# Two expert ranks fixed after two of four batches, their weights prepared beside the third mixing, units handed out three times, and their rows loaded by plain transfers

## The chip, the cores and the metric

The kernel runs on one core of a Trainium2 chip. The metric is the device time of one execution in microseconds (us); the median of three runs is shown below. An engine is a part of the core with an instruction queue of its own, worked off strictly in order: PE multiplies matrices, DVE and ACT do elementwise work, POOL issues transfers with lists of row numbers (indirect transfers), SP issues plain transfers and transposing transfers. An engine whose next instruction waits holds everything queued behind it.

## The reference

Two stages. The first is an attention over channels, for 4 batches of 5056 tokens and 256 channels; the second is a mixture of 8 experts in which each token goes to the one expert with the largest gate.

```python
qn = q / (norm(q, axis=1) + 1e-6);  kn = k / (norm(k, axis=1) + 1e-6)   # B=4, N=5056, C=256
s = kn.transpose(0, 2, 1) @ qn / tau          # 256 x 256 for each batch
a = softmax(s, -1);  x = v @ a                # rows of x are the 20224 tokens
e_idx = argmax(x @ w_gate, 1)                 # one of 8 experts for each token
out[mask] = gate_w * sigmoid(x @ w_output_gate)[e] * (relu(x[mask] @ w1[e]) @ w2[e])   # mask: e_idx == e
```

w1 is 8 x 256 x 1024 and w2 is 8 x 1024 x 256. The experts' load is known only once the gates are computed.

## The kernel before

**Gram and mixing.** For each batch, `gram` loads q and k in tiles of 128 x 512 (tile `qk`, six buffers), multiplies them into `s_ps` (L341), adds up squares (ACT L328, DVE L329), and ends in a short softmax. `mix` then goes through the batch in 5 groups of 4 steps: each step turns a tile of v on PE (`vt_ps`, L456), copies it out (`vh` on ACT L460, `vl` on DVE L462) and multiplies (`x_ps`, L479 to L481; copied to `st` by ACT L482). A group has 16 turned blocks (of 128 x 128) and 48 products of `x_ps`. After a group, `route` picks the expert of each token with some 18 small DVE instructions, counts places with nine small PE products (`r_ps`, L540 and L543), and scatters the 1024 rows by eight indirect transfers (POOL L559) into `xs_d`, a list in DRAM with a region for each expert. `rc` holds the number of tokens that each expert has so far.

**Weights.** `prep` fetches an expert's weights by indirect transfer (`raw`, POOL L245, 1 MB for w1 and 1 MB for w2, called halves here), in the order of rank: rank 0 is the expert with the most tokens when the ranks are fixed. `split` takes the square (ACT L268, two pieces into the buffer of `whi`), sums it on PE (`w_ps`, L273), makes a scale from it (DVE), and writes a high part `whi` (ACT L290, four pieces for w1 and two for w2) and a low part `wlo` (DVE L291), which SP stores to `wsc` in DRAM (L297).

**Units.** A unit is 256 tokens (or 128) of one expert. `table` lays down for each unit where its rows lie (`gi`) and which weight rows it needs (`wi`). `open_marks` reads a mark behind the scatters, so that `gi` is known only when they have landed. `fetch_x` loads a unit's rows (`xg`, L781), `fetch_w` its weights (`wbuf`, L768, 1 MB for each half, two buffers), `prepare` scales the rows (ACT L826, DVE L827) and has SP transpose them (`xt`, L831). PE multiplies 48 times for the first layer (`h_ps`, L850 to L852; out by ACT L854 and DVE L855 to `hb`) and 48 times for the second (`y_ps`, L873 to L875); ACT writes `yo`, POOL scatters it to the output (L885). There are 72 whole units and 21 halves.

**Order.** The main part interleaves generators: `_beside(main, (gen, rate))` makes `rate` steps of `gen` for each of `main`. The order of each engine's queue then comes from a scheduler that weighs the instructions of these steps. Before the change: the grams run beside the mixings of batches 0 to 2; after the third mixing the ranks are fixed and 10 units handed out, and ranks 0 and 1 are prepared beside the first 14 steps of the last mixing; the units start beside its end; after it the other 83 units are handed out and ranks 2 to 7 prepared beside the units.

```python
for b in range(B - 1):
    _beside(mix(b), (ahead, GRATE))
early = checkpoint(False)
next(early)
preps = prep(0, 2, "raw")
tail = mix(B - 1)
```

Of the kernel before, what the change touches and what calls it, by code (L numbers as in the profile page):

```python
# [20 lines left out]
P = 128  # L21
# [5 lines left out]
def _beside(main, *others):  # L27

    due = [0.0 for _ in others]
    for _ in main:  # L30
        for i, (gen, rate) in enumerate(others):
            due[i] += rate
            while due[i] >= 1.0:
                due[i] -= 1.0
                next(gen, None)


@with_exitstack
def tile_colnorm_attention_then_top1_moe(
# [37 lines left out]
    EARLY = 10  # L77
# [5 lines left out]
    SURE = -(-((B - 1) * N - E * (BLK - 1)) // BLK)  # L83
    FIRST = [-(-r * SURE // E) for r in range(E)]
    assert EARLY <= FIRST[2] and EARLY + LATER - NHALF >= FIRST[E - 1]
# [32 lines left out]
    PRATE = 1  # L118
    ALONE = 14
    LATE = 7  # L120
    BRATE = 1.0
    WRATE = 0.45
# [70 lines left out]
    mark = cst.tile([P, 2], I32, name="mark")  # L193
# [42 lines left out]
    def prep(first, end, tag):  # L236
        todo = []
        for r in range(first, end):
            for half in range(2):
                if tag == "st":  # L240
                    raw = wk.tile([P, R, CW], F32, tag="st", name=f"raw{r}_{half}", bufs=STB)
                    raw = raw.rearrange("p r w -> p (r w)")[:, :HW1]
                else:
                    raw = big.tile([P, HW1], F32, tag="raw", name=f"raw{r}_{half}", bufs=3)
                nc.gpsimd.indirect_dma_start(  # L245
                    out=raw,
                    out_offset=None,
                    in_=wraw[half],
                    in_offset=bass.IndirectOffsetOnAxis(ap=ri[:, r : r + 1], axis=0),
                    bounds_check=E * P - 1,  # L250
                    oob_is_err=False,
                )
                todo.append(lambda raw=raw, half=half, r=r: split(raw, half, r))
                yield
                if len(todo) > 1:
                    yield from todo.pop(0)()
        for f in todo:
            yield from f()
# [175 lines left out]
    def mix(b):  # L434
# [5 lines left out]
        def turn(j):  # L440
# [20 lines left out]
            vl = wk.tile([P, CC, 2 * P], F32, tag="vl", name="vl", bufs=XTB).bitcast(F32R)  # L461
# [236 lines left out]
    def rank_experts():  # L698
# [288 lines left out]
```

## Time and profile before

| what | value |
|---|---|
| median of three runs (lowest, highest) | 1265.51 us (1261.57, 1273.47) |
| the profiled execution | 1272.18 us, of which the profile's span is 1270.5 us |
| granted PE clock over the span | 0.98 |
| PE busy | 1204.7 us (95%), 10708 matmul records |
| DVE, ACT, POOL busy | 735.6, 629.5, 655.8 us |
| bytes moved | 211.46 MB, mean 166 GB/s |

The span begins with the first instruction. The grams and the first three mixings run to about 286 us, the last mixing and the first units to about 400 us, and units fill the rest. A record is one pass through PE: a product of `s_ps` has two, the other large ones one.

### The profile page before, as it was taken

How to read it: one execution, taken by the hardware profiler on the slowest of the kernel's cores; microseconds unless marked ns; L12 is line 12 of the kernel's file. 1: busy time of each engine (PE TensorE's matmuls, PEld its weight loads, DVE VectorE, ACT ScalarE, POOL GpSimd, SP SyncE). 2: the span in 40 equal slices, each digit the busy share in tenths (PEclk: the TensorE clock that was granted, in tenths of full speed). 3: DMA queues.
4: the chain of work that ended last, by engine and by line, in shares of the span. 5: the costliest groups of instructions: out<-in, count | busy, mean ns of one | idle time of the engine just before them, and what ended most of it. 6: DMA issues, size and time to landing. Idle time of an engine off the chain costs nothing.

```text
span 1270.5 us, 28599 instructions
## 1 busy us (share of the span) xinstructions
PE 1204.7 (95%) x10708; PEld 1092.5 (86%) x10708; DVE 735.6 (58%) x2235; ACT 629.5 (50%) x1231; POOL 655.8 (52%) x643
## 2 busy tenths in 40 slices
PE   7999999996669999999999999899999999999996
PEld 6899898995668788888888888788899999999996
DVE  5767767766678466565656666444445555555431
ACT  4676666664755456455554645333333444334332
POOL 0005665667577754555555544344455555555442
PEclk9999999998879999999999999999999999999999
DMA  9877787857697765565565546933263333465520
GB/s 333 277 251 243 244 276 230 270 179 228 218 329 181 190 159 167 120 143 144 144 143 144 143 111 159 180 70 73 64 176 107 78 78 79 114 212 165 161 59 17
DMA packets 176418, 211.46 MB, mean 166 GB/s; under 512 B 125352, under 2 KB 127022, under 8 KB 171032
## 3 DMA queue, kind: packets, MB, share of 16 engines
q1 hardware_dynamic: 124568, 100.73, 29.4%
q0 software_dynamic: 51712, 108.92, 29.3%
q8 instruction: 84, 1.38, 0.5%
q14 instruction: 54, 0.44, 0.1%
HBM read 296.94 MB, written 61.80 MB: 282 GB/s over the span
## 4 chain that ended last, share of the span: by engine, by line
PE 81%; DMA 9%; DVE 3%; ACT 2%; issue 2%; POOL 1%; SPq 0%; POOLq 0%; ACTq 0%; DVEq 0%
PE h_ps L850 10%; PE h_ps L852 10%; PE h_ps L851 10%; PE y_ps L875 10%; PE y_ps L873 10%; PE y_ps L874 10%; PE s_ps L341 9%; DMA qk<-in_k_dram 3%; PE x_ps L479 3%; PE x_ps L480 2%; PE x_ps L481 2%; DMA xg<-xs_d,gi 2%; PE vt_ps L456 2%; DMA xs_d<-st,r_si 1%; DMA raw<-in_moe_w_dram,ri 1%
## 5 line engine op out<-in xcount | busy, mean ns | idle before, releaser
L850 PE MATMUL h_ps<-xt,wbuf 128*128 128x256 f16 (+1 forms) x1488 | 376.5, 262 | 7.4 <-DMA wbuf<-wsc,wi 5.2
L851 PE MATMUL h_ps<-xt,wbuf 128*128 128x256 f16 (+1 forms) x1488 | 376.5, 262 | 0.0
L852 PE MATMUL h_ps<-xt,wbuf 128*128 128x256 f16 (+1 forms) x1488 | 376.4, 262 | 0.0
L855 DVE SCALAR_TENSOR_TENSOR hb<-h_ps,hb 128x512 f16<-128x512 f32 (+1 forms) x372 | 232.3, 628 | 238.4 <-ACT hb L854 237.1
L875 PE MATMUL y_ps<-wbuf,hb 128*128 128x256 f16 x1320 | 360.1, 273 | 5.0 <-DVE hb L855 5.0
L873 PE MATMUL y_ps<-wbuf,hb 128*128 128x256 f16 x1320 | 360.0, 273 | 0.8 <-ACT hb L854 0.8
L874 PE MATMUL y_ps<-wbuf,hb 128*128 128x256 f16 x1320 | 360.0, 273 | 0.0
L854 ACT ACTIVATE hb<-h_ps 128x512 f16<-128x512 f32 (+1 forms) x372 | 199.7, 545 | 314.3 <-PE h_ps L852 310.6
L768 POOL DMA_INDIRECT wbuf<-wsc,wi x186 | 188.1, 1011 | 290.3 <-PE h_ps L852 242.4
L559 POOL DMA_INDIRECT xs_d<-st,r_si x160 | 177.0, 1106 | 194.8 <-ACT st L482 119.3
L885 POOL DMA_INDIRECT out_dram<-yo,b_id x165 | 168.4, 1021 | 60.4 <-issue 43.9
L850 PEld LDWEIGHTS <-wbuf 128*128 128x128 f16 x1488 | 147.1, 99 | 23.0 <-DMA wbuf<-wsc,wi 7.7
L851 PEld LDWEIGHTS <-wbuf 128*128 128x128 f16 x1488 | 146.2, 98 | 14.4
L341 PE MATMUL s_ps<-qk 128*128 128x256 f32 x640 | 150.3, 385 | 8.5 <-DMA qk<-in_k_dram 7.8
L852 PEld LDWEIGHTS <-wbuf 128*128 128x128 f16 x1488 | 146.3, 98 | 13.8
L875 PEld LDWEIGHTS <-hb 128*128 128x128 f16 x1320 | 129.2, 98 | 20.6 <-DVE hb L855 5.6
L874 PEld LDWEIGHTS <-hb 128*128 128x128 f16 x1320 | 129.2, 98 | 14.9 <-issue 0.9
L873 PEld LDWEIGHTS <-hb 128*128 128x128 f16 x1320 | 129.3, 98 | 14.0
L341 PEld LDWEIGHTS s_ps<-qk 128*128 128x128 f32 x640 | 119.5, 193 | 23.4 <-DMA qk<-in_q_dram 8.2
L826 ACT ACTIVATE xr<-xg,b_sx 128x256 f16<-128x256 f32 x165 | 75.6, 500 | 99.1 <-DMA xt<-xr 69.9
L329 DVE TENSOR_TENSOR acc<-acc,sq 128x1024 f32<-128x1024 f32 x76 | 93.0, 1224 | 52.4 <-ACT sq L328 43.8
L827 DVE SCALAR_TENSOR_TENSOR xr<-xg,b_sx,xr 128x256 f16<-128x256 f32 x165 | 74.0, 481 | 84.2 <-ACT xr L826 80.5
(187 smaller groups left out, 1603.8 us busy)
## 6 DMA issues: line engine op xcount, KB each, us to landing
qk<-in_q_dram SPq DMA_DIRECT2D x76, 256.0 KB
qk<-in_k_dram SPq DMA_DIRECT2D x76, 256.0 KB
v<-in_v_dram SPq DMA_DIRECT2D x32, 512.0 KB
wsc<-whi SPq DMA_DIRECT2D x16, 512.0 KB
wsc<-wlo SPq DMA_DIRECT2D x16, 512.0 KB
v<-in_v_dram SPq DMA_DIRECT2D x8, 480.0 KB
wbuf<-wsc,wi POOLq DMA_INDIRECT x186
xt<-xr SPq DMA_TRANSPOSE x165
```

The lines of the kernel that those rows point to most:

```text
L341: nc.tensor.matmul(s_ps[:, c, :], kt[:, 1, t, c * P : (c + 1) * P], qt[:, 0, t, :], start=st == 0 and t0 == 0 and t == 0 and c == 0 and n ...
L559: ins = nc.gpsimd.indirect_dma_start(out=xs_d[:, :], out_offset=bass.IndirectOffsetOnAxis(ap=si[:np_, t : t + 1], axis=0), in_=st[:np_, t, ...
L768: nc.gpsimd.indirect_dma_start(out=wbuf[half][:, u % NW, :], out_offset=None, in_=wsc[half][:end, :], in_offset=bass.IndirectOffsetOnAxis( ...
L850: nc.tensor.matmul(hp, w1s[:, 0, c, fs], xh, start=fi == 0 and c == 0, stop=False, **KWM)
L851: nc.tensor.matmul(hp, w1s[:, 0, c, fs], xl, start=False, stop=False, **KWM)
L852: nc.tensor.matmul(hp, w1s[:, 1, c, fs], xh, start=False, stop=fin, **KWM)
L854: nc.scalar.activation(hh, h_ps[:, :, :w], AF.Relu)
L855: nc.vector.scalar_tensor_tensor(out=hb[:, 1, 2 * fp : 2 * fp + 2, :w], in0=h_ps[:, :, :w], scalar=0.0, in1=hh, op0=ALU.max, op1=ALU.subtract,
L873: nc.tensor.matmul(y_ps[:, t, :], hb[:, 0, f, tsl], w2s[:, 0, f, :], start=st, stop=False, **KWM)
L874: nc.tensor.matmul(y_ps[:, t, :], hb[:, 0, f, tsl], w2s[:, 1, f, :], start=False, stop=False, **KWM)
L875: nc.tensor.matmul(y_ps[:, t, :], hb[:, 1, f, tsl], w2s[:, 0, f, :], start=False, stop=fin, **KWM)
L885: ins = nc.gpsimd.indirect_dma_start(out=out[:, :], out_offset=bass.IndirectOffsetOnAxis(ap=un["id"][:, t : t + 1], axis=0), in_=un["yo"][ ...
```

## The change

Of `prep`, `split`, the hand-outs and the main part:

- Ranks 0 and 1 are fixed when two batches are mixed (`rank_experts(False)`), and ranks 2 to 7 when three are (`rank_experts(True)` keeps the first two).
- Units are handed out three times: 8 after two batches, 10 after three, 75 after all four. Units 0 to 3 are of rank 0 by construction (`FIRST` is 0, 4, 8, 16, 23, 30, 38, 45), so units 2 and 3 fetch no weights.
- Ranks 0 and 1 are prepared beside the third mixing, which still has the fourth gram beside it; the first units are opened from its 17th step. The fourth mixing then runs with units and with the preparation of ranks 2 to 7 beside it.
- `whi` and `wlo` have one buffer each where they had two. Up to three halves of raw weights are fetched ahead.
- A unit's rows are loaded by SP with a plain transfer. Its address is read from `gi` into a register of SP (`values_load`), so POOL has no transfer for it any more.
- The transposed rows `xt` have buffers of their own, which they shared with `vl`.

```diff
+    FEW = (8, 10)
+    EARLY = sum(FEW)
+    SOON, AHEAD = 2, 2
...
-    PRATE = 1
-    ALONE = 14
-    LATE = 7
-    BRATE = 1.0
-    WRATE = 0.45
+    PRATE = 1.6
+    DEEP, LAG, REST = 3, 4, 2
+    LATE, OPEN = 5, 16
+    FAR, NEAR = 3, 2
+    BRATE = 0.8
+    WRATE = 0.8
...
-    def prep(first, end, tag):
+    def prep(first, end):
+        jobs = [(r, half) for r in range(first, end) for half in range(2)]
+        raws = []
+
+        def gather():
+            r, half = jobs[len(raws)]
+            if r > AHEAD:
+                raw = wk.tile([P, R, CW], F32, tag="st", name=f"raw{r}_{half}", bufs=STB)
+                raw = raw.rearrange("p r w -> p (r w)")[:, :HW1]
+            else:
+                raw = big.tile([P, HW1], F32, tag="raw", name=f"raw{r}_{half}", bufs=3)
...
+        for n, (r, half) in enumerate(jobs):
+            while len(raws) < min(n + DEEP, len(jobs)):
+                gather()
                 yield
+            yield from pause(LAG if n == 0 else REST)
+            yield from split(raws[n], half, r)
...
-        hi = big.tile([P, HW1], F16, tag="sp", name=f"whi{r}_{half}")
-        lo = big.tile([P, HW1], F16, tag="sl", name=f"wlo{r}_{half}")
+        hi = big.tile([P, HW1], F16, tag="sp", name=f"whi{r}_{half}", bufs=1)
+        lo = big.tile([P, HW1], F16, tag="sl", name=f"wlo{r}_{half}", bufs=1)
...
     def fetch_w(half, u):
+        if NW <= u < FIRST[1]:
+            return
...
-        ins = nc.gpsimd.indirect_dma_start(
...
+        at = nc.values_load(
+            un["gi"][0:1, :], engines=[mybir.EngineType.SP], min_val=0, max_val=rows.shape[0] - P,
...
+        ins = nc.sync.dma_start(
+            out=xg[:, : un["nt"], :].rearrange("p t w -> p (t w)"), in_=rows[bass.ds(at, P), :]
         )
...
-        xt = wk.tile([P, CC, 2 * P], F32, tag="vl", name="xt", bufs=XTB)
+        xt = wk.tile([P, CC, 2 * P], F32, tag="xt", name="xt", bufs=XTB)
...
-    for b in range(B - 1):
+    for b in range(SOON):
         _beside(mix(b), (ahead, GRATE))
...
+    some = checkpoint(0)
+    next(some)
+    preps = prep(0, AHEAD)
+    for b in range(SOON, B - 1):
+        for i, _ in enumerate(_steps(mix(b), (ahead, GRATE), (preps, PRATE))):
+            if i == LATE:
+                finish(some)
+            if i >= OPEN:
+                next(run)
...
+    finish(preps)
+    some = checkpoint(1)
+    next(some)
+    preps = prep(AHEAD, E)
+    for i, _ in enumerate(_steps(mix(B - 1), (run, BRATE), (preps, BRATE * WRATE))):
         if i == LATE:
-            finish(early)
...
+    finish(checkpoint(2))
+    _beside(run, (preps, WRATE))
```

ACT's queue where the first weights are split, before; `raw_0_3880` and `raw_1_3909` are the two halves of rank 0:

```order
L268 ACTIVATE whi_0_3940,wss<-raw_0_3880 128x1024 x2
L482 COPY st_1_4004<-x_ps 128x272
L268 ACTIVATE whi_1_4261,wss<-raw_1_3909 128x1024 x2
L460 CAST vh<-vt_ps 128x512
L482 COPY st_1_4004<-x_ps 128x272
L290 ACTIVATE whi_0_3940<-raw_0_3880,wsw 128x512 x4
```

And now, in the third mixing; `raw_0_2824` and `raw_1_2863` are the halves of rank 0, `sq_19` is the last square of the fourth gram:

```order
L284 ACTIVATE whi_0_3014,wss<-raw_0_2824 128x1024 x2
L476 CAST vh<-vt_ps 128x512 x2
L498 COPY st_1_2987<-x_ps 128x272 x2
L306 ACTIVATE whi_0_3014<-raw_0_2824,wsw 128x512 x4
L498 COPY st_2_3276<-x_ps 128x272
L344 ACTIVATE sq_19_0_3436<-qk_19_3429 128x1024
L539 ACTIVATE r_d<-r_d 128x64
L498 COPY st_2_3276<-x_ps 128x272
L476 CAST vh<-vt_ps 128x512
L498 COPY st_2_3276<-x_ps 128x272 x2
L284 ACTIVATE whi_1_3354,wss<-raw_1_2863 128x1024 x2
```

The second half's square now stands behind the first half's scaling, and it writes the buffer that the first half's store reads from.

SP's queue around the first store of weights, before (`v_4_0` and `v_4_2` are the last tiles of v of a batch):

```order
L450 DMA v_4_0_4564<-in_v_dram 120x1024
L450 DMA v_4_2_4790<-in_v_dram 120x1024
L297 DMA wsc_85<-whi_0_3940 128x2048
L297 DMA wsc_85<-wlo_0_3941 128x2048
L297 DMA wsc_86<-whi_1_4261 128x2048
L297 DMA wsc_86<-wlo_1_4262 128x2048
L831 DMA_TRANSPOSE xt<-xr_4653 128x4x128 x2
```

And now (`TENSOR_LOAD gi` reads an address into a register; it and the two rows after it stand three times ahead of the store, shown once):

```order
L466 DMA v_4_0_3587<-in_v_dram 120x1024
L807 TENSOR_LOAD gi
L811 ISA
L811 DMA xg<-xs_d 128x544
...
L313 DMA wsc_85<-whi_0_3014 128x2048
L313 DMA wsc_85<-wlo_0_3015 128x2048
L466 DMA v_4_2_3738<-in_v_dram 120x1024
```

Before, all loads of v stood ahead of the stores. Now the stores, the units' rows and the loads of v of the third and fourth mixing alternate in one queue; the store of the second half (`whi_1_3354`) has four transposes and two loads of v of the fourth mixing ahead of it.

PE's queue at the first product of a unit, before (`v_2_2`, `v_3_0` and so on have all been turned by then):

```order
L543 MATMUL r_ps<-r_oh,onesb 128x16
L273 MATMUL w_ps<-wss,onesf 128x1
L543 LDWEIGHTS onesb
L543 MATMUL r_ps<-r_oh,onesb 128x8
L850 LDWEIGHTS wbuf_158
L850 MATMUL h_ps<-xt,wbuf_158 128x256
```

And now:

```order
L472 MATMUL vt_ps<-ident,v_1_2_4312 128x128 x4
L495 MATMUL x_ps<-ah_3930,vh 128x272
L496 MATMUL x_ps<-al_3931,vh 128x272
L497 MATMUL x_ps<-ah_3930,vl 128x272
L875 LDWEIGHTS wbuf_158
L875 MATMUL h_ps<-xt,wbuf_158 128x256
```

Before, all 80 turned blocks of the fourth batch and 180 of its 240 products of `x_ps` stood ahead of the first unit. Now 32 blocks and 36 products do, and the rest is spread among the first four units.

More of the change, by code (lines that the diff above doesn't have):

```diff
@@ L27, in _beside, with _steps @@
 def _beside(main, *others):
+    for _ in _steps(main, *others):
+        pass
+def _steps(main, *others):
     due = [0.0 for _ in others]
@@ L234, in tile_colnorm_attention_then_top1_moe @@
     prepped = []
-    def prep(first, end, tag):
[L237 to L253, printed above, removed]
+    def prep(first, end):
[8 more added lines that the diff above has]
+                raw = big.tile([P, HW1], F32, tag="raw", name=f"raw{r}_{half}", bufs=3)
+            nc.gpsimd.indirect_dma_start(
+                out=raw,
+                out_offset=None,
+                in_=wraw[half],
+                in_offset=bass.IndirectOffsetOnAxis(ap=ri[:, r : r + 1], axis=0),
+                bounds_check=E * P - 1,
+                oob_is_err=False,
+            )
+            raws.append(raw)
+        for n, (r, half) in enumerate(jobs):
+            while len(raws) < min(n + DEEP, len(jobs)):
+                gather()
@@ L707, in rank_experts @@
         nc.vector.scalar_tensor_tensor(out=key, in0=key, scalar=float(E), in1=c8, op0=ALU.mult, op1=ALU.add)
+        for r in range(AHEAD if again else 0):
+            nc.vector.scalar_tensor_tensor(
+                out=key, in0=rank[:, r, :], scalar=float((E - r) * NTOK), in1=key, op0=ALU.mult, op1=ALU.add
+            )
         above = sm.tile([P, E, E], F32, tag="tb_rk", name="tb_above")
@@ L727, in checkpoint @@
         else:
-            rank_experts()
+            rank_experts(ck > 0)
         of_rank(rcr, rc)
-        open_marks(int(last))
+        open_marks(ck)
         yield
         if not last:
-            table(int(last), BLK, EARLY, lambda a: [(a[:, :EARLY], lambda r: r)])
-            weights(0, EARLY)
-            new = [2] * EARLY
+            a = len(units)
+            z = a + FEW[ck]
+            table(ck, BLK, FEW[ck], lambda row: [(row[:, a:z], lambda r: r)])
+            weights(a, z)
+            new = [2] * FEW[ck]
         else:
@@ L751, in halves @@
                 return [(grid[:, :, s], lambda r: r)]
-            table(int(last), BLK, LATER, fulls)
-            table(int(last), BLK // 2, NHALF, halves)
+            table(ck, BLK, LATER, fulls)
+            table(ck, BLK // 2, NHALF, halves)
             weights(EARLY, NUNIT)
@@ L780, in fetch_x @@
         xg = xg.rearrange("p a t c -> p (a t c)").bitcast(I32)[:, : 2 * CW].rearrange("p (t w) -> p t w", t=2)
-        ins = nc.gpsimd.indirect_dma_start(
-            out=xg[:, : un["nt"], :].rearrange("p t w -> p (t w)"),
-            out_offset=None,
-            in_=xs_v[un["nt"]],
-            in_offset=bass.IndirectOffsetOnAxis(ap=un["gi"], axis=0),
-            bounds_check=xs_v[un["nt"]].shape[0] - 1,
-            oob_is_err=False,
+        rows = xs_v[un["nt"]]
+        at = nc.values_load(
+            un["gi"][0:1, :], engines=[mybir.EngineType.SP], min_val=0, max_val=rows.shape[0] - P,
+            skip_runtime_bounds_check_because="slots of the table lie in the regions or are the rows behind them",
+        )
+        ins = nc.sync.dma_start(
+            out=xg[:, : un["nt"], :].rearrange("p t w -> p (t w)"), in_=rows[bass.ds(at, P), :]
         )
@@ L913, in blocks @@
             if g == 0:
-                yield
+                yield from pause(FAR)
+                for n in range(1 + XP):
+                    adv("prep", prepare, n + 1)
+                    yield
+                yield from pause(NEAR)
             adv("prep", prepare, g + 1)
```

42 lines of the change are left out of this document (17 added, 25 removed).

## The prediction, made before the changed kernel was timed

> **What bounds the kernel now.** I read the page's slices first, then the same 40 slices as a table by engine, then the chain of waits and the instructions of each engine around the gap.
>
> ```profile
> PE   7999999996669999999999999899999999999996
> PEclk9999999998879999999999999999999999999999
> DMA  9877787857697765565565546933263333465520
> 254.10:285.90 31.80, 31.80 (x245) 30.39 (x244) 19.40 (x72) 19.25 (x44) 19.68 (x20) 1.00 0.56 179
> 285.90:317.60 31.70, 20.25 (x172) 18.83 (x171) 20.66 (x99) 13.61 (x40) 23.42 (x25) 0.87 0.70 228
> 317.60:349.40 31.80, 20.81 (x154) 19.96 (x154) 20.40 (x79) 23.30 (x47) 19.01 (x17) 0.82 0.64 219
> 349.40:381.10 31.70, 22.19 (x165) 19.97 (x166) 24.47 (x100) 17.94 (x33) 24.05 (x23) 0.72 1.05 329
> 381.10:412.90 31.80, 29.72 (x276) 26.31 (x274) 28.03 (x119) 17.21 (x38) 24.79 (x24) 1.00 0.76 181
> 412.90:444.70 31.80, 28.72 (x247) 24.85 (x248) 15.20 (x40) 14.41 (x24) 24.52 (x25) 0.95 0.76 190
> 444.70:476.40 31.70, 30.03 (x277) 26.73 (x276) 21.73 (x78) 16.21 (x32) 18.51 (x19) 1.00 0.62 159
> 476.40:508.20 31.80, 31.80 (x294) 28.55 (x293) 21.38 (x57) 19.26 (x35) 15.46 (x16) 1.00 0.57 167
> 794.10:825.80 31.70, 26.72 (x230) 22.98 (x229) 14.17 (x37) 10.31 (x22) 12.59 (x12) 0.95 0.94 181
> ```
>
> A row of the table gives the stretch, its length, the busy time (and records) of PE, PE's weight loads, DVE, ACT and POOL, the granted clock, the share of the DMA engines and GB/s. PE is full nearly everywhere but in six slices from 285.9 to 476.4, the fourth mixing and the first units, and in one at 794. In the six it idles 11.45 + 10.99 + 9.51 + 2.08 + 3.08 + 1.67 = 38.8 us, and in three of them its clock is down.
>
> To include the clock I count the work at PE's full pace, which these rows of the chain give (start, us, what):
>
> ```profile
> 255.92 0.44 PE vt_ps L456 x4
> 257.37 0.13 PE x_ps L481
> 257.50 0.13 PE x_ps L479
> 257.88 1.73 PE s_ps L341 x8
> ```
>
> A turned block takes 0.11 us; the 12 products of `x_ps` between 256.36 and 257.88 take 0.127 each; a record of `s_ps` takes 0.216, a whole product 0.43; and 294 unit products in 31.8 us take 0.108 each. The 1291 records from 285.9 to 476.4 are, in the queue's order, 246 of `x_ps` (31.2 us), 79 turned blocks (8.7), 878 unit products (94.9) and small ones (about 6). That is 141 us of work in 190.5: the gap costs **49 us**, 10 of them by the clock. No more is to be had by this change, since PE is full before and behind it.
>
> ```profile
> 794.77 15.20 DMA xg<-xs_d,gi
> ```
>
> The slice at 794 loses 4.98 us, and 0.05 of 26.7 us, 1.3, to the clock: a transfer of a unit's rows took 15.2 us there. The profiled execution took 1272.18 us, and without these 6.3 it is 1265.9, the median (1265.51). I take it for an accident of this execution, and subtract it when I come to the median.
>
> **What makes the gap.** The third mixing ends, the ranks are fixed, and the first unit waits for a chain through every engine:
>
> ```profile
> 310.77 1.00 POOL L559 DMA_INDIRECT xs_d<-st,r_si  x1 [0.30 <-issue]
> 312.07 1.05 POOL L245 DMA_INDIRECT raw<-in_moe_w_dram,ri  x1 [0.30 <-DVE wi L689]
> 312.07 6.27 DMA raw<-in_moe_w_dram,ri
> 318.36 1.06 ACT L268 ACTIVATE whi<-raw 128x1024 f16<-128x1024 f32 x1 [6.30 <-DMA raw<-in_moe_w_dram,ri]
> 319.56 0.59 PE w_ps L273 x2
> 324.87 4.66 ACT L290 ACTIVATE whi<-raw,wsw 128x512 f16<-128x512 f32 x4
> 329.56 0.35 SPq L297 DMA_DIRECT2D wsc<-whi  x1
> 330.77 0.34 SPq L297 DMA_DIRECT2D wsc<-wlo  x1
> 339.27 2.19 ACT L290 ACTIVATE whi<-raw,wsw 128x1024 f16<-128x1024 f32 x2
> PEld w_ps L273 <- ACT whi L268: 20.3, 2, 11.2
> ```
>
> Scatters hold POOL to 311.77, the gather takes 6.3 us, ACT squares, PE sums, ACT scales, SP stores. PE stood before the sums 20.3 us in two waits, since its queue is in order. No gram is left to fill in.
>
> **The change, part by part.**
>
> *The chain begins earlier.* The second mixing's last scatters end on POOL at 249.75 in the profile, and its queue is the same up to there:
>
> ```profile
> 248.75 1.00 POOL L559 DMA_INDIRECT xs_d<-st,r_si  x1 [0.30 <-issue]
> 249.16 0.20 PE L540 MATMUL r_ps<-r_oh,tri 128*128 128x64 bf16 x1
> ```
>
> Before, PE's first sum came 319.56 - 311.77 = 7.8 us after POOL was free; the same delay gives 257.5. PE's place for it: the counting products of the following group, which started at 249.16, now have 5 more products of `s_ps` ahead (2.2 us), and from them to the sum stand 5 more `s_ps` and 8 turned blocks (3.5 with the counting): 254.8. PE waits 2.7 us. But q and k still stream in then; if these halve the gather's rate, its flight of 6.27 - 1.05 = 5.2 us doubles and the wait is 7.9. I take **5**, between the ends. The Trainium skill (DMA: Bandwidth & Descriptors, on queues, rings and completion order) says that a DMA engine takes turns between its queues packet by packet. By that rule the upper end holds, and the sum below is 3 us longer; no row here shows a gather beside loads of q and k.
>
> *Four halves are split one behind the other.* From the first sum to the seventh (the fourth half) PE's new queue holds 16 `s_ps`, 64 turned blocks, 156 `x_ps` and small ones: 6.9 + 7.0 + 19.8 + 6 = 40 us. Three halves have to go by in these 40 us, or PE waits at the next sum. A half's time, p, runs from its square to the next: with one buffer, the next square waits until the store of `whi` has landed. From the square at 318.36 to the store's issue at 329.56 are 11.2 us; the landing is bounded by these rows:
>
> ```profile
> 302.93 2.44 DMA xs_d<-st,r_si
> 216.84 5.32 DMA qk<-in_k_dram
> L482 ACT COPY st<-x_ps 128x272 f32<-128x272 f32 x160 | 59.2, 391 | 22.6 <-PE x_ps L481 17.5 <-DMA xs_d<-st,r_si 3.7
> L460 ACT CAST vh<-vt_ps 128x512 fp32r<-128x512 f32 x80 | 46.5, 588 | 14.5 <-PE vt_ps L456 8.4 <-PE x_ps L480 5.3
> L826 ACT ACTIVATE xr<-xg,b_sx 128x256 f16<-128x256 f32 x165 | 75.6, 500 | 99.1 <-DMA xt<-xr 69.9 <-DMA out_dram<-yo,b_id 9.9 <-DVE b_sx L212 7.6
> SPq L450 <- PE vt_ps L456: 74.2, 20, 7.8
> SPq L831 <- DVE xr L827: 23.9, 10, 6.2
> ```
>
> So p is 13.6 (2.4 us) to 16.9 (5.3 with the issue's 0.35), if ACT and SP are free. They are not. ACT's queue from the first to the fourth square has 26 copies of `st` (10.2), 15 of `vh` (8.8), 12 scalings of units' rows (6.0), six pieces of squares (6.3) and ten of scaling (4.66 + 2.19 + 4.66 = 11.5): 42.8 us, with the fourth batch's softmax on top, so p is at least 14.3 on average. And the store stands on SP behind loads of v and transposes, whose longest waits were 7.8 and 6.2 us; with the first of them p reaches 24.7. I take p = 17.5, nearer to the lower end, since ACT's load is the row that surely applies: 3 x 17.5 - 40 = **12.5 us** late at the fourth half. The ends are 1 and 34.
>
> *The fourth mixing with units beside it.* PE is no longer short of work. What stays is the end of it, where POOL's scatters alternate with fetches of weights: the last two slices of the gap lost 3.08 + 1.67 idle and 1.4 by the clock, **6 us**. POOL now has no transfers of rows there, but the same scatters and weights. The ends are 0 and 12, twice the row. The new marks (one more) and the second ranking are some 40 small DVE instructions beside a mixing: nothing, unless DVE waits for the mark.
>
> *Rows by SP.* POOL loses 93 transfers, SP gains as many, with a register load each:
>
> ```profile
> L781 POOL DMA_INDIRECT xg<-xs_d,gi x93 | 100.3, 1078 | 35.5 <-issue 13.4 <-DVE hb L855 6.9 <-DVE b_iv L814 6.4
> 789.27 2.50 SPq L831 DMA_TRANSPOSE xt<-xr  x2
> ```
>
> POOL is idle half the time in full slices (15.46 of 31.8), so 100.3 us less is worth nothing there. SP has 2.5 us of transposes in the 96 x 0.108 = 10.4 us of a unit. A register load is not in the profile: bounded by an SP issue (0.35) and POOL's 1.08, it is hidden. Were it above 7 us, each unit would pay the rest. The four weight fetches left out, of 186, are hidden too, as is the faster preparation of ranks 2 to 7: in the full slice at 476 ACT has 12.5 and DVE 10.4 us free.
>
> *Sum.* Of the gap's 49 us come back as waits 5 + 12.5 + 6 = 23.5. The profiled execution would take 1272.18 - 25.5 = 1246.7, and without the accident at 794 1240.4. I predict **1240**. With the clock's share as before (10 in 38.8 idle) already in the last term but not in the first two, up to 4 us more are possible. The Trainium skill (TensorE: Matmul & The Clock Gate, on the clock gate) has PE at half rate until it has been busy some 3.4 us. By that rule, three waits cost 3 x 1.7 = 5 us, and the sum is 1245; the slice at 794, with 1.3 us for 4.98 idle, agrees.
>
> **Rivals.** (a) *All is hidden.* p is 13.6 and the first wait 2.7: 2.7 + 0.8 + 0 to 6 comes back, 1220 to 1226. For it: SP's stores went out 0.03 us after the scaling before. Against it: ACT's 42.8 us in a stretch of 40. (b) *Little is gained.* One wait of SP's queue per half, p near 24.7: 5 + 34 + 6 = 45, 1262. For it: the second store has two loads of v and four transposes ahead. (c) *Slower, by SP's queue and the single buffer.* Both of SP's waits fall on every half: p = 16.9 + 7.8 + 6.2 = 30.9, and 5 + 52.7 + 6 = 63.7 come back: 1280.6. It gains nothing from p = 26, and is slower by 1% from p = 30.2. Against it: such waits came to a mean of 3.7 (74.2 by 20) and 2.4 us.
>
> **How the numbers follow.** The forecast (11 to 36 us come back, 1228 to 1253) has 0.5; (a) 0.2; (b) 0.18; (c) 0.12. A measurement of this kernel can tell about 1% from no change, 12.7 us: faster means below 1252.9. That is (a) and 0.95 of the forecast, 0.67; slower is (c) but for its lower edge, 0.11; the rest, 0.22, is within 1%. The range leaves out the lowest of (a), 0.05, and (c) with the top of (b), 0.15: 1221 to 1268.
>
> **What would show it.** In the changed profile the first weight sum on PE should be near 255 to 263, with a wait on ACT's square; the three next pairs of squares some 17 us apart, their waits on the store of `whi`; ACT 90% busy or more between 255 and 310; the first unit's product at 305 to 325 instead of 362; PE full from about 440. Squares 14 us apart without waits would be (a); 25 or more, with SP's stores queued behind v or transposes, (b) or (c). Wrong altogether would be a slower steady state, with unit after unit waiting for `xt` behind SP's register loads, or the gram's products waiting for q and k in the third mixing.

## The result, and the profile after

The changed kernel took 1277.18 us (median of 12 runs, 1273.12 to 1284.01), the kernel before 1267.07 (12 runs, 1261.57 to 1273.57): a ratio of 1.008, 95% interval 1.006 to 1.0099. It is 10 us slower, where 25 us less were forecast. Its profiled execution took 1280.97 us (span 1279.3).

Three rows of the page's 40 slices, and the slices of the gap as a table by engine (stretch, length, busy time and records of PE, weight loads, DVE, ACT and POOL, granted clock, share of the DMA engines, GB/s), with the first stretch of four halves as one row more:

```profile
PE   7999999995888889999999999999999999999996
PEclk9999999997878989999999999999999999999998
DMA  9877787889862577675754444833254343465520
254.00:285.80 31.80, 27.79 (x181) 25.77 (x182) 22.54 (x83) 22.08 (x43) 14.92 (x14) 0.89 0.86 284
285.80:317.50 31.70, 17.97 (x121) 16.31 (x120) 25.25 (x100) 23.21 (x50) 17.62 (x16) 0.78 1.09 316
317.50:349.20 31.70, 28.72 (x234) 27.43 (x234) 23.87 (x115) 16.64 (x38) 20.29 (x20) 0.89 0.78 270
349.20:381.00 31.80, 25.08 (x170) 21.09 (x168) 14.57 (x48) 12.22 (x29) 11.60 (x12) 0.79 0.73 163
381.00:412.80 31.80, 27.93 (x222) 24.82 (x221) 12.88 (x48) 10.57 (x26) 15.32 (x17) 0.89 0.32 95
412.80:444.50 31.70, 30.06 (x284) 26.96 (x284) 25.10 (x102) 19.80 (x40) 22.35 (x22) 1.00 0.45 125
444.50:476.20 31.70, 25.25 (x215) 21.86 (x213) 19.63 (x73) 12.43 (x23) 20.07 (x20) 0.89 0.81 231
250.00:310.00 60.00, 42.72 (x275) 38.67 (x273) 43.72 (x174) 37.93 (x75) 33.17 (x32) 0.86 0.97 299
```

(The share of the DMA engines is the time that packets took over the time of 16 engines; in one slice it comes to more than 1.) The deep hole of three slices has gone, and a shallow one from 254 to 476 has come. The same kind of table with one stretch for all of it, of the kernel before and then of the changed one:

```profile
250.00:480.00 230.00, 191.22 (x1589) 174.08 (x1588) 156.86 (x603) 125.69 (x266) 157.14 (x150) 0.91 0.72 212
```

```profile
250.00:480.00 230.00, 189.07 (x1463) 169.62 (x1462) 149.38 (x581) 120.75 (x250) 126.95 (x122) 0.88 0.71 212
```

PE is busy 2 us less, but gets through 126 records fewer. Placed in the queue's order and counted at full pace, as in the prediction, PE's records lose 62.0 us of these 230 to waits and slow pace, where they lost 46.6 before: 15.4 more. Hardly any of it is idle time: PE is idle 230 - 189.07 = 40.9 us now and was idle 38.8. The rest is slow pace, 21.1 us now and 7.8 before. At 794, where the execution before lost 6.7 us by this count, the changed one loses 1.3. Together that is 10.0 us more, near the 10.1 between the medians and the 8.8 between the two profiled executions.

PE's longer waits, from the changed kernel's timeline (start, us, instruction; in brackets the wait and what ended it), with the first unit product:

```profile
255.38 0.58 PE L289 MATMUL w_ps<-wss,onesf 128*128 128x1 f32 x2 [2.92 <-ACT whi L284]
298.33 1.19 PE L395 MATMUL n_ps<-dq,onesf 128*128 128x256 f32 x2 [6.11 <-DVE r_oh L536]
301.79 0.58 PE L289 MATMUL w_ps<-wss,onesf 128*128 128x1 f32 x2 [2.27 <-ACT whi L284]
312.00 0.39 PE L495 MATMUL x_ps<-ah,vh 128*128 128x272 f32 x1 [3.32 <-ACT st L498]
323.12 0.58 PE L289 MATMUL w_ps<-wss,onesf 128*128 128x1 f32 x2 [2.98 <-ACT whi L284]
331.82 0.28 PE L875 MATMUL h_ps<-xt,wbuf 128*128 128x256 f16 x1
364.75 1.11 PE L472 MATMUL vt_ps<-ident,v 128*128 128x128 f32 x4 [2.87 <-DVE vl L478]
392.10 0.60 PE L495 MATMUL x_ps<-ah,vh 128*128 128x272 f32 x1 [3.23 <-ACT st L498]
451.75 0.40 PE L875 MATMUL h_ps<-xt,wbuf 128*128 128x256 f16 x1 [6.45 <-DVE tb_ok L701]
```

Weight sums (L289) are three of them. (One wait of 2.57 us, for ACT's `hb` at 352.75, is left out.) The longest of the third mixing is the first product of the fourth batch's softmax (L395), for which PE had to wait for DVE, and at 451.75 a unit waits for DVE's last hand-out.

### The profile page after: what moved, and what is told of

Same layout as the page of the kernel before. It is cut to its first block, busy times and chain, and to the rows that moved or that the text cites. A ratio compares the mean times of both kernels' runs of the same rounds, so it can differ in the third digit from the quotient of the medians.

```text
span 1279.3 us, 28755 instructions
## 1 busy us (share of the span) xinstructions
PE 1215.4 (95%) x10708; PEld 1100.3 (86%) x10708; DVE 735.2 (57%) x2280; ACT 630.5 (49%) x1231; POOL 555.4 (43%) x547
## 4 chain that ended last, share of the span: by engine, by line
PE 71%; DMA 10%; issue 9%; POOL 4%; ACT 2%; DVE 2%; SPq 1%; POOLq 0%; ACTq 0%; DVEq 0%
PE h_ps L875 9%; PE h_ps L876 9%; PE h_ps L877 9%; PE y_ps L898 9%; PE y_ps L899 9%; PE y_ps L900 9%; PE s_ps L357 8%; DMA qk<-in_k_dram 3%; PE x_ps L495 2%; PE x_ps L496 2%; PE x_ps L497 2%; POOL out_dram L910 2%; DMA wbuf<-wsc,wi 2%; PE vt_ps L472 2%; POOL wbuf L793 1%
## 5 line engine op out<-in xcount | busy, mean ns | idle before, releaser
L495 PE MATMUL x_ps<-ah,vh 128*128 128x272 f32 x320 | 108.4, 339 | 12.1 <-ACT st L498 9.8
```

## The experiments

The runs fell on several chips; the record numbers five, and they form two groups. On three (8, 2 and 1) the kernel before took 1265.65 to 1266.9 us in the sets of runs, close to the 1267.07 of the result above, whose chip has no number on record; these are called the first group. On the other two (0 and 3, the second group) it took 1373 to 1378. Each ratio is to the kernel before on the same chip in the same set, and runs of different sets are compared by these ratios. The letters are theories: (A) the single buffer of `whi`; (B) SP's queue with units' rows and transposes; (C) the preparation of ranks 2 to 7 beside the fourth mixing; (D) the register loads; (E) the units' preparation in the third mixing, on all engines; (F) the chain of halves itself; (G) full transfer engines.

For the runs of the first group this is what PE's records lost, in us, counted as above. Counted by each record's own start instead, an entry moves by up to 3 us and a sum by up to 2; the entry below nothing shows the same.

| kernel | 250 to 330 | 330 to 410 | 410 to 480 | sum |
|---|---|---|---|---|
| before | 18.9 | 20.0 | 7.7 | 46.6 |
| changed | 34.1 | 19.1 | 8.8 | 62.0 |
| changed, again | 33.4 | 18.3 | 9.3 | 61.0 |
| ranks 2 to 7 later | 34.2 | 2.3 | 11.2 | 47.7 |
| the same, two buffers of `whi` | 29.8 | 1.7 | 12.2 | 43.7 |
| ranks 2 to 7 later, units opened later | 32.9 | 15.4 | 5.6 | 53.9 |
| the same, two buffers of `whi` | 32.7 | 13.2 | 2.5 | 48.4 |
| the first hand-out read later | 24.6 | 18.3 | -0.4 | 42.5 |
| ranks 2 to 7 later, third buffer of `xr` | 31.5 | 5.6 | 11.4 | 48.5 |

### First set, on the second group of chips: parts undone one at a time

Two buffers for `whi`:

```diff
-        hi = big.tile([P, HW1], F16, tag="sp", name=f"whi{r}_{half}", bufs=1)
+        hi = big.tile([P, HW1], F16, tag="sp", name=f"whi{r}_{half}", bufs=2)
```

> The changed kernel with two buffers for whi (wlo keeps one). Theory A (the single buffer under full DMA engines): the third half's square waited until 300.58 us for the store of whi, which was issued at 290.00 and took 10.51 us to land; with a second buffer the four squares come about 14 to 18 us apart (17.96, 28.44 and 21.36 before), the seventh weight sum on PE near 305 instead of 323, and the kernel is 8 to 12 us faster than the changed one (0.991 to 0.994 of it). Theory B (SP's queue, with the units' transposes in the third mixing, holds stores and units back): the squares move up, but PE's 6.1 us at the fourth softmax stay, and 0 to 4 us are gained. Theory C (the second preparation beside the fourth mixing costs the most): 0 to 4 us here, since the stretch from 330 to 440 us stays as it is.

Ranks 2 to 7 prepared later, and then faster:

```diff
-    preps = prep(AHEAD, E)
+    preps = chain(pause(11), prep(AHEAD, E))
...
-    _beside(run, (preps, WRATE))
+    _beside(run, (preps, 1.2))
```

> The changed kernel with ranks 2 to 7 prepared from about the 17th step of the fourth mixing on, instead of its first. Theory C: in the changed kernel three gathers of 1 MB stand ahead of the second mark on POOL, so the mark lands 11.1 us after its issue, ACT stands 4.7 us for raw with PE's hb behind it, and a raw tile holds one of the three buffers of st, so that ACT waits 4.85 us for a scatter; PE loses about 20 us from 330 to 440 us. Without these, 8 to 15 us are gained. Theories A and B: the loss lies ahead of 330 us; 0 to 4 us are gained.

The first units opened behind the third mixing:

```diff
-    LATE, OPEN = 5, 16
+    LATE, OPEN = 5, 99
```

> The changed kernel with the first units opened with the fourth mixing instead of the 17th step of the third. Theory B: no transposes and no rows of units on SP and DVE in the third mixing, so the stores of weights go out when they are written, the 6.1 us at the fourth softmax go, and the stretch up to 330 us loses some 10 us less; but the first unit's product comes later than 331.8 us, and what is saved there may be paid again: minus 8 to plus 3 us. Theory A: the third square still waits for the landing of whi, and the units come later: 0 to 6 us slower.

The units' rows by POOL again:

```diff
-        at = nc.values_load(
...
-        ins = nc.sync.dma_start(
+        ins = nc.gpsimd.indirect_dma_start(
```

> The changed kernel with the units' rows loaded by POOL's indirect transfers again. Theory D (the register load on SP holds the queue until the row numbers are known, and everything behind it): SP's waits at the rows (34.6 us in 3, with 20.2 the longest) go, and 5 us or more are gained. Theories A to C: those waits are not ahead of anything that is late, and the time is within 3 us of the changed kernel; POOL, with 93 transfers of 1.08 us more, may make it 1 or 2 us slower.

Measured, beside 1374.56 us before: 1340.61 (0.974, 0.970 to 0.978), 1337.81 (0.973, 0.970 to 0.976), 1348.42 (0.982, 0.978 to 0.986), and with the rows by POOL 1395.03 (1.014, 1.011 to 1.018). This was chip 0. The changed kernel itself, run later on chip 3, took 1343.00 (0.975, 0.968 to 0.982, beside 1378.37). So on this group the change gains, the first three edits move little, and rows by POOL cost some 50 us: there the move to SP is worth 3.9% within the changed kernel, and the rest of the change costs 1.4%. What sets this group apart are waits for which the profile finds no releaser in the core ("remote"). From the table of waits, first with the rows by POOL and then of the changed kernel (engine, what it was about to write, us in all, times, longest):

```profile
ACT hb L880 <- remote: 137.2, 47, 7.2
```

```profile
ACT hb L879 <- remote: 58.2, 28, 6.5
```

No profile of the first group has such a row. I can't say what they wait for. The disputed time is that of the first group, on which the next runs fell.

### On the first group: what costs the ten microseconds

The changed kernel once more, unchanged: 

> The changed kernel itself, unaltered, as the measure for what runs beside it: the four kernels before ran on a chip where the kernel before took 1374.6 us instead of 1267, so each variant needs the changed kernel on its own chip. If the chips differ in everything alike, its ratio to the kernel before stays 1.008; if the slower chip stretches waits, the ratio may be anywhere from 0.98 to 1.02, and on a chip like the first one it is 1.006 to 1.010.

1278.40 us beside 1266.04, 1.0086 (1.0048 to 1.0124): the result stands.

Ranks 2 to 7 later and two buffers of `whi` (both edits from above): 

> The changed kernel with both edits of the first call: two buffers for whi, and ranks 2 to 7 prepared from about the 17th step of the fourth mixing on. Theory A (single buffer under full DMA engines) and theory C (the second preparation beside the fourth mixing) price different stretches, ahead of 330 us and behind it: if both hold, the gains add up to 16 to 25 us against the changed kernel, and it is faster than the kernel before by 0.5 to 1%. If only one holds, 6 to 12 us against the changed kernel, and it is level with the kernel before.

The kernel before with the units' rows by SP, nothing else of the change: 

> The kernel before with one part of the change alone: the units' rows loaded by SP with a register's address; ranks, hand-outs and buffers as before. The prediction took this as hidden: within 3 us of the kernel before. Theory D (SP's register loads hold its queue): 5 us or more slower, since the rows' loads stand on SP ahead of the stores of weights. If POOL's 93 transfers did cost time after all, it is faster by up to 10 us.

```diff
-        ins = nc.gpsimd.indirect_dma_start(
+        at = nc.values_load(
...
+        ins = nc.sync.dma_start(
```

1266.38 us, 0.9995 (0.9969 to 1.0021), and 1266.82, 1.0008 (0.9979 to 1.0037). The rows by SP cost nothing here, which ends (D), and the two edits together win the ten microseconds back. To part them:

Ranks 2 to 7 later, alone: 

> The kernel of e2 (only the preparation of ranks 2 to 7 moved later) once more, beside the two kernels below, so that the two edits of e6 are told apart. Theory C alone: all of e6's gain is in it, 1263 to 1269 us, with the work at PE's full pace some 10 to 25 us less behind between 330 and 410 us. Theory A (the second buffer of whi did its share): 1270 to 1275 us.

The same with units opened later: 

> The kernel of e8, and the first units opened with the fourth mixing instead of the third's 17th step. Theory E (the units' preparation in the third mixing, where the transfer engines are full, holds the queues: a transposing transfer stood on SP for 5.5 and 8.3 us instead of 1.25, ACT stood 8.1 us for its buffer, and the fourth softmax on DVE came 6.1 and 12.5 us late for PE): the softmax' wait goes, the stretch 250 to 330 us loses 10 to 20 us less, and, if the later first unit does not cost it again, 1250 to 1260 us. Theory F (the halves themselves are late there, units or not): the stretch loses as much as before, and the units come later: 1266 to 1276 us.

And with both and two buffers of `whi`: 

> The kernel of e9 with two buffers for whi. With no transposes on SP between the stores, the single buffer may now be what the squares wait for. Theory A: the four squares come 3 to 18 us apart and 3 to 8 us are gained against e9. Theory E: the stores land soon enough, and it is within 3 us of e9.

1268.18 us, 1.0006 (0.9976 to 1.0036); 1279.92, 1.0079 (1.004 to 1.0117); 1270.55, 1.0019 (0.9997 to 1.0041); all beside 1266.90. Preparing ranks 2 to 7 later (and then faster) is by itself worth the ten microseconds, and the table says where: from 330 to 410, 2.3 us lost in place of 19.1. (C) stands for this group of chips; on the second the same edit took 0.973 of the kernel before against 0.975, no clear gain. In the chain of waits, first of the changed kernel and then of this run, the mark behind the third mixing's scatters (start, us, what):

```profile
345.53 11.14 DMA mark<-xs_d
```

```profile
346.30 2.66 DMA mark<-xs_d
```

Two gathers of weights stand ahead of the changed kernel's mark on POOL (341.75 and 343.09 us) and none just ahead of the other run's. ACT meanwhile waits for the weights of rank 2, and later for a buffer of `st`, of which the raw weights of rank 3 hold one (gathered at 346.43). How much each of the three costs was not tested apart. From its timeline:

```profile
350.03 1.06 ACT L284 ACTIVATE whi<-raw 128x1024 f16<-128x1024 f32 x1 [4.74 <-DMA raw<-in_moe_w_dram,ri]
391.66 0.96 ACT L498 COPY st<-x_ps 128x272 f32<-128x272 f32 x3 [4.85 <-DMA xs_d<-st,r_si]
```

Two slices of the run with ranks 2 to 7 later, beside which the changed kernel had 25.08 and 27.93 at clocks of 0.79 and 0.89:

```profile
349.20:381.00 31.80, 28.24 (x252) 25.68 (x251) 20.71 (x77) 16.54 (x41) 18.11 (x18) 1.00 0.52 156
381.00:412.80 31.80, 31.15 (x288) 28.46 (x288) 16.70 (x68) 14.02 (x33) 22.50 (x23) 1.00 0.64 169
```

(A) fell as the cause: a second buffer moved nothing beside this edit (0.9995 against 1.0006, on chips 8 and 2) nor alone on the second group (0.974 against 0.975, on chips 0 and 3). It did bring 9.4 us with units opened later, of which the table places 5.5; the rest stays open, as does why opening later costs 11.7 us, outside both forecasts of its time. That edit also told less than I wanted of (B) and (E): the rows and transposes of units stayed where they were in SP's queue, from 267 and 280 us on. (B) by itself stays untested.

### The units' preparation in the third mixing

The mark of the first hand-out read at step 14 and its table laid at step 17, so that no rows are loaded or transposed before the third mixing's end, on top of the two later edits:

```diff
+        if ck == 0:
+            yield
...
-            if i == LATE:
+            if i == 14:
+                next(some)
+            if i == 17:
                 finish(some)
```

> The kernel of e9, and the first mark read behind the scatters of the third mixing's 14th step, with the units of the first hand-out laid down at the 17th. In e9 the units were opened later in the code, but their rows (from 267 us) and transposes (from 280 us) kept their place beside the third mixing in SP's queue, so e9 said nothing on theory E. Here the row numbers are not known before, and no rows, transposes or weights of units can stand there. Theory E (the units' preparation beside the third mixing fills the transfer engines and holds SP, ACT and DVE, so that the fourth softmax comes late): the softmax' wait (4.1 to 15.5 us in e6 to e10) goes, the stretch 250 to 330 us loses 10 to 20 us less than e8's 34, and the kernel takes 1250 to 1260 us, unless the units then come too late for the end of the fourth mixing. Theory F (splitting the four halves there costs it, units or not): the stretch loses 25 us or more, and the kernel takes 1266 to 1280 us.

Three buffers for `xr` and the gram's squares, beside ranks 2 to 7 later:

```diff
-        xr16 = wk.tile([P, 2, 2, C], F32, tag="sq", name="xr16").bitcast(F16)[:, :, 0, :]
+        xr16 = wk.tile([P, 2, 2, C], F32, tag="sq", name="xr16", bufs=3).bitcast(F16)[:, :, 0, :]
```

> The kernel of e8 with three buffers instead of two for the scaled rows (tag sq), which a transposing transfer reads from. Theory E in its narrow form (ACT stands for that buffer, 1.7 us in the changed kernel and 8.1 and 10.3 us in e6 and e10, and DVE and the softmax with it): the softmax' wait shrinks to 2 us or less and 3 to 8 us are gained, 1260 to 1265 us. If the transfers themselves are late, with the engines full, the wait only moves to the next buffer or to the rows: within 3 us of e8's 1268.

1269.49 us, 1.0028 (1.0009 to 1.0047), and 1272.33, 1.0048 (1.0016 to 1.008), beside 1265.65. The third buffer gains nothing. The later hand-out's time is the one that (F) forecast, and its stretch of 24.6 us lies on the border of both forecasts. Still it shows part of (E) at work: the halves of weights then go by without the units. ACT's squares in the changed kernel's timeline, and then in this run's:

```profile
254.18 1.06 ACT L284 ACTIVATE whi<-raw 128x1024 f16<-128x1024 f32 x1 [4.90 <-DMA raw<-in_moe_w_dram,ri]
272.14 1.06 ACT L284 ACTIVATE whi<-raw 128x1024 f16<-128x1024 f32 x1 [1.29 <-DMA wsc<-whi]
300.58 1.06 ACT L284 ACTIVATE whi<-raw 128x1024 f16<-128x1024 f32 x1 [2.81 <-DMA wsc<-whi]
321.94 1.04 ACT L284 ACTIVATE whi<-raw 128x1024 f16<-128x1024 f32 x1
```

```profile
255.27 1.06 ACT L284 ACTIVATE whi<-raw 128x1024 f16<-128x1024 f32 x1 [6.87 <-DMA raw<-in_moe_w_dram,ri]
269.16 1.06 ACT L284 ACTIVATE whi<-raw 128x1024 f16<-128x1024 f32 x1 [1.01 <-DMA wsc<-whi]
287.87 1.06 ACT L284 ACTIVATE whi<-raw 128x1024 f16<-128x1024 f32 x1 [0.58 <-DMA wsc<-whi]
307.40 1.06 ACT L284 ACTIVATE whi<-raw 128x1024 f16<-128x1024 f32 x1 [3.46 <-DMA wsc<-whi]
```

Apart by 17.96, 28.44 and 21.36 us with the units (mean 22.6), by 13.89, 18.71 and 19.53 without (mean 17.4). From 250 to 330 PE loses 24.6 us in place of the 32.9 with the units there, in the run that differs by this edit alone (units opened later); against that run the time falls from 1.0079 of the kernel before to 1.0028. But the units' work isn't saved: the first products come later, 330 to 410 loses 18.3, in place of 15.4 with units opened later and of 2.3 with ranks 2 to 7 later alone, and against the last of these nothing is gained.

### Are the transfer engines full?

In the slice at 285.8 the share of the DMA engines is 1.09, so I loaded them further: behind each load of v for the third mixing but the first, the tile loaded before it is also stored to a spare place (nine transfers of 0.5 MB, 4.7 MB, that nothing reads):

```diff
+                if b == 2 and "v" in sts:
+                    nc.sync.dma_start(spare[2 * g + i // 2], sts["v"])
```

In the changed kernel: 

> The changed kernel with nine extra transfers in the third mixing: behind each load of v the tile before it is also copied to a spare place in DRAM (9 times 0.5 MB, 4.7 MB; the outputs are as before). Theory G (the transfer engines are full from 250 to 330 us, 289 GB/s with a share of 0.97 and more, so that each byte more is time): at 290 to 350 GB/s 4.7 MB are 13 to 16 us, and the changed kernel is 10 to 16 us slower than 1278. Theory F (the chain of halves is late for its own steps, with capacity to spare): 0 to 4 us slower.

In the kernel before: 

> The kernel before with the same nine extra transfers at the same place. Its third mixing has a transfer share of 0.56 and 179 GB/s in the slice at 254 us, so both theories expect little: 0 to 3 us slower. If it is slower by 8 us or more, the extra transfers cost by their place in SP's queue or by q and k of the fourth gram, and e13 says nothing on the full engines.

The changed kernel with the later hand-out, two buffers of `whi`, and `LAG` at 9 in place of 4, so that the split begins later: 

> The kernel of e11 with two buffers for whi and the first split five steps later, so that PE's first sum (it waited 4.8 us) and the squares (they waited 1.0, 0.6 and 3.5 us for a store's landing) find their data. Theory F: 5 to 9 us faster than e11's 1269.5, 1260 to 1265, which would be the first version faster than the kernel before. Theory G: the waits move to the next transfer: within 4 us of e11.

These fell on the second group (chip 3), beside 1373.31 us: 1346.01 (0.979, 0.975 to 0.984), 1378.84 (1.004, 1.001 to 1.007) and 1348.01 (0.980, 0.977 to 0.983). The kernel before got some 5 us slower by the bytes, where 0 to 3 were expected, and the later split is no better than the changed kernel. For lack of the unchanged kernel there the bytes were run again beside it, with the last variant: the later hand-out and two buffers, the later rate of 1.2, `PRATE` at 1.0, and the halves spread over both mixings:

```diff
-    PRATE = 1.6
+    PRATE = 1.0
...
-    finish(preps)
...
-    preps = prep(AHEAD, E)
-    for i, _ in enumerate(_steps(mix(B - 1), (run, BRATE), (preps, BRATE * WRATE))):
+    preps = chain(preps, pause(3), prep(AHEAD, E))
+    for i, _ in enumerate(_steps(mix(B - 1), (run, BRATE), (preps, 1.0))):
```

Halves spread: 

> The kernel of e11 with two buffers for whi, and the four halves of ranks 0 and 1 spread: one step of their preparation for each step of a mixing (1.6 before), going on into the fourth mixing instead of being finished ahead of it. Theory G (full transfer engines): with fewer bytes in 250 to 330 us the stretch loses 10 us less than e11's 25, the fourth mixing takes the rest of them beside its own work, and the kernel is 5 to 12 us faster than e11: 1257 to 1264 us, where e11 took 1269.5 beside 1265.7 for the kernel before. Theory F: four waits at PE's weight sums as before, only later, and the units later too: 1268 to 1276 us.

The extra bytes: 

> The kernel of e13 once more (the changed kernel with 4.7 MB more in the third mixing). Theory G: 10 to 16 us slower than the changed kernel beside it (e18). Theory F: 0 to 4 us slower.

The changed kernel beside them: 

> The changed kernel unaltered, as the measure for e17 on the same chip. On a chip like the first one 1.006 to 1.010 of the kernel before; on the chip of e1 to e4, by their trend (0.973 to 0.982 with three different edits), 0.98 to 0.99.

1321.89 us (0.963, 0.955 to 0.971), 1342.89 (0.978, 0.970 to 0.985) and 1343.00 (0.975, 0.968 to 0.982), beside 1378.37. The stretch from 250 to 330 us with the extra bytes and without:

```profile
250.00:330.00 80.00, 63.24 (x391) 58.08 (x389) 54.72 (x216) 46.58 (x97) 42.91 (x40) 0.81 0.94 308
```

```profile
250.00:330.00 80.00, 62.37 (x403) 57.32 (x402) 55.58 (x230) 46.31 (x95) 41.65 (x38) 0.88 0.90 286
```

In the changed kernel the bytes cost nothing that four runs of each show. But that says little against (G). SP issues the loads of v ahead of the mixing, so that six of the nine stores went out from 203.91 to 245.56 us and only three in the stretch that was to be loaded; its rate rose by 22 GB/s, which is 1.8 MB. And this group's share of the DMA engines from 250 to 310 was 0.84 to begin with, where the first group's was 0.97. On the first group it wasn't tried. (G) stays open.

Spreading the halves is the best version that was run, 21 us below the changed kernel on the second group. Its gain isn't in the gap. From 480 to 800, first with halves spread and then the changed kernel beside it:

```profile
480.00:800.00 320.00, 318.44 (x2923) 285.39 (x2921) 194.72 (x535) 170.91 (x309) 135.19 (x127) 1.00 0.56 136
```

```profile
480.00:800.00 320.00, 300.15 (x2701) 264.34 (x2702) 195.23 (x583) 165.15 (x296) 137.90 (x134) 0.97 0.59 145
```

It gets through 222 more records there, of 0.108 us each: 24 us. ACT's "remote" waits at `hb` in this stretch are 3.8 us in 2, and 25.0 in 9 in the changed kernel, so the gain may belong to this group of chips; its cause isn't shown. This version did not run on the first group. The variants that did are at best level with the kernel before.

## Why the prediction was wrong

**What bounds the kernel.** Right: all of the difference lies in the gap and at 794. PE is full behind 480 in both, and the accident at 794 did not come again.

**The chain begins earlier.** Right. The first sum came at 255.38 us (255 to 263 forecast) behind ACT's square, which waited 4.90 us for the gather. PE waited 2.92 and lost 4.3 in all up to 260; 5 was the term. Its upper end, a gather at half its rate beside q and k, did not come: the gather took 6.69 us, and 6.27 in the kernel before.

**Four halves one behind the other.** The term, 12.5, was mis-sized: from 260 to 330 PE lost 29.8 us. With p = 22.6 in place of 17.5 its formula gives 27.8. So p was too small: it had ACT's load and SP's stores in it, and the units' twelve scalings, but not the waits that the units bring into the queues. The run without them has p = 17.4. The difference shows in the changed kernel's timeline of SP, and behind it in two pieces of its chain of waits:

```profile
279.58 8.86 SPq L856 DMA_TRANSPOSE xt<-xr  x3
```

```profile
290.00 10.51 DMA wsc<-whi
304.72 6.54 DMA xt<-xr
```

Three transposes hold SP 8.9 us; the store of `whi` behind them then takes 10.5 to land, against the 2.4 to 5.3 of my bounds, in the slice with the DMA engines' share at 1.09; and the third square starts 28.4 us after the second. Meanwhile DVE's part of the softmax holds PE for 6.11 us. In the run with ranks 2 to 7 and units later and two buffers, scaling a unit's rows stood on ACT for a transpose, and the softmax came 15 us late:

```profile
307.50 1.93 ACT L851 ACTIVATE xr<-xg,b_sx 128x256 f16<-128x256 f32 x4 [10.33 <-DMA xt<-xr]
311.80 1.19 PE L395 MATMUL n_ps<-dq,onesf 128*128 128x256 f32 x2 [15.46 <-DVE r_se L542]
```

The forecast sign "ACT 90% busy" failed with it: ACT was busy 37.93 of 60 us, 63%. Queues that wait, not load, set p. Two more signs failed: the first unit's product came at 331.82 us (305 to 325 forecast), and PE was full from about 460 us, not 440.

But p isn't the whole of this term. The formula counts one thing, how late PE comes to the last sum. At the later weight sums PE stood only 2.27 and 2.98 us; the softmax's 6.11, 3.32 for a buffer of `st` and slow pace are the rest. In the run with two buffers of `whi` and ranks 2 to 7 later, p is 17.3 with the units still there, from the first and the last of the four squares, and the softmax takes the place of the halves:

```profile
255.69 1.06 ACT L284 ACTIVATE whi<-raw 128x1024 f16<-128x1024 f32 x1 [5.45 <-DMA raw<-in_moe_w_dram,ri]
307.69 1.06 ACT L284 ACTIVATE whi<-raw 128x1024 f16<-128x1024 f32 x1 [2.30 <-DMA wsc<-whi]
305.93 1.19 PE L395 MATMUL n_ps<-dq,onesf 128*128 128x256 f32 x2 [12.51 <-DVE r_oh L536]
```

From 250 to 330 it loses 29.8 us, in place of 34.2 without the second buffer. So a p as forecast would not have brought the forecast time. That the result is near rival (c), 1280.6, is luck: p never came to 30.9 on average, and the loss behind 330 isn't in it.

A large part is the clock, which the prediction left at up to 4 us. Even with p = 17.4 the run of the later hand-out loses 24.6 us from 250 to 330, where the terms give 5 + 12.2 = 17.2. Products of `x_ps` behind the first wait, from the changed kernel's timeline, and the stretch behind that wait as a row of the table by engine:

```profile
256.20 0.43 PE L496 MATMUL x_ps<-al,vh 128*128 128x272 f32 x1
256.42 0.43 PE L497 MATMUL x_ps<-ah,vl 128*128 128x272 f32 x1
254.70:261.50 6.80, 6.12 (x25) 5.94 (x26) 1.50 (x4) 3.39 (x8) 0.00 (x0) 0.50 0.94 315
```

They start 0.22 us apart, where 0.127 is the full pace, and the granted clock is 0.50 for 6.8 us. The changed kernel has nine waits of 2 us or more between 250 and 480, the kernel before six, with about the same time in them (32.7 and 31.8 us): more and shorter waits. The trace's clock records have eight such spells at half clock in these 230 us, each beginning in or just behind one of the nine waits, six of them at waits of only 2.57 to 3.32 us; in the kernel before there were four. At half clock, half of PE's busy time is lost: 21.8 us in these spells, where it was 10.2, so 11.6 of the 15.4 us. The Trainium skill (TensorE: Matmul & The Clock Gate, "What's actually happening") gives a cold clock until a window of some 3.4 us has been busy; the 6.8 us agree with two such windows. By that rule the prediction would have come to 1245, which is the right way and far too little: it reckoned with three waits, where nine came.

**The fourth mixing.** "PE is no longer short of work" is the step that made the kernel slower rather than level. Its cost was put at nothing but for the end; PE lost 19.9 us from 330 to 440. Ten microseconds of the kernel's time are the preparation of ranks 2 to 7 beside this mixing; by the rows above their gathers delay the mark, ACT waits for them in order, and their raw weights hold a buffer that the mixing's scatters need. The run with ranks 2 to 7 later shows the price, 1.0006 of the kernel before in place of 1.0086. I had read the cover from the full slice at 476, where no mixing runs.

The term for the end, 6, was right in size (8.4 from 440 to 460) and wrong in mechanism. It isn't POOL's scatters against fetches of weights but the third hand-out on DVE, ahead of a unit's `hb`:

```profile
447.86 1.87 DVE L613 MEMSET void<- 128x2176 int32 x1 [5.21 <-DMA xs_d<-st,r_si]
```

It clears a buffer of `st`, and waits until a scatter has left it. With ranks 2 to 7 later PE still waits for DVE near there, though the clearing (414.36 us) waited only 1.35 us, and for no scatter:

```profile
423.67 0.37 PE L875 MATMUL h_ps<-xt,wbuf 128*128 128x256 f16 x1 [4.50 <-DVE hb L880]
```

**Rows by SP.** Right on the first group: the kernel before with this edit alone is the same, and units never wait for it: all waits of PE from 480 to 1240 us in the changed kernel are 1.9 us, for weights. Its table of PE's waits there, and the register loads on SP (shortest, median and longest in ns):

```profile
PE y_ps L898 <- DMA wbuf<-wsc,wi: 1.3, 1, 1.3
PE h_ps L875 <- DMA wbuf<-wsc,wi: 0.6, 1, 0.6
```

```profile
L807 SPq TENSOR_LOAD <-gi x93: 268/489/1170, 263.6 to 1180.6; - x93
```

At 0.27 to 1.17 us a register load lies about within the bounds, 0.35 to 1.08. What went wrong with units is not their loads but where their transposes and scalings stand.

**The sum.** 4.3 + 29.8 + 19.9 + 8.4 = 62.4 us came back where 23.5 was forecast; the gap lost 46.6 by the same count. Three steps failed: the term of the four halves (29.8 for 12.5), the fourth mixing put at nothing (19.9), and, spread over both, the clock, left at up to 4 us where some 21 of the 62 are slow pace.

What stays open: why 42 to 54 us are still lost in all variants on the first group, where edits that took a loss from one stretch gave part of it to another; and why the second group stands where the first doesn't.

## What to carry to other kernels

Moving a waiting chain beside other work costs that work's queues: count for every instruction moved not its duration but the longest wait that it may stand in its in-order queue, and what stands behind it. Free time of an engine is to be read from the stage in which the work will run, and a buffer shared between the moved work and that stage is a wait of its own. One long hole cut into several short ones saves less than their lengths say: here idle time stayed near 40 us, and half the clock behind the waits cost some 12 us more.

## What was unexpected of the hardware

- A transpose can hold SP's queue far longer than its median. Of the 165 transposes of the changed kernel the median is 1.26 us; in the crowded stretch one took 5.5 us (all of the kernel; shortest, median and longest in ns), 8.3 with ranks 2 to 7 later and two buffers, and 9.2 with units opened later as well:

```profile
L856 SPq DMA_TRANSPOSE xt<-xr x165: 1189/1257/5515, 277.0 to 1232.6; - x165
```

- A wait of 2.57 us is all that stands ahead of one spell at half clock (from 353.70 us, for 3.4 us), and six of the eight spells at half clock began at waits of 2.57 to 3.32 us.
- Two groups of chips gave the kernel before 1266 and 1374 us, 8.5% apart, and opposite signs of the change: 1.008 on one, 0.975 on the other. On the slower one engines stand in waits that no row explains, fewer of them with the rows of units by SP.
